# Loading a channel-mixing matrix as fp32 through SyncE in pieces of eight partitions, and rounding it on VectorE

## The chip, the core and the metric

The kernel runs on one core of one Trainium2 chip. The metric is the device time of one execution in microseconds (us). The kernel before takes 434.22 us, the median of three runs (433.93 to 435.81).

## What is computed

Two parts follow one another. The first is causal attention over 8 batches, 8 heads, 576 positions and 64 channels per head. Heads 0 to 3 see the last 32 positions, heads 4 to 7 every 32nd position. The second part takes the result as `x` (8 x 576 x 512), mixes its first 64 Fourier modes with one complex 512 x 512 matrix per mode, and then mixes channels with one real matrix, `w_ch`:

```python
X = np.fft.rfft(x, axis=1)                       # along the 576 positions
Yr = einsum('bmd,mde->bme', Xr, w_r) - einsum('bmd,mde->bme', Xi, w_i)
Yi = einsum('bmd,mde->bme', Xr, w_i) + einsum('bmd,mde->bme', Xi, w_r)
y = np.fft.irfft(Y, n=S, axis=1)                 # 64 modes, the others are zero
u = x + y
out = u + np.maximum(u @ w_ch, 0.0)
```

All inputs are fp32. `w_r` and `w_i` are 64 x 512 x 512 each, 64 MiB each. `w_ch` is 512 x 512, 1 MiB.

## The kernel before

The mode matrices are by far the largest input. They are fetched in halves of 256 input channels. One call fetches a half of two modes: two transfers issued by GpSimd, one for the real and one for the imaginary matrices, each of which reads 1 MiB of fp32 and writes 512 KiB of fp16 (the transfer rounds).

```python
GUEST = {1: "Y0", 2: "X0", 7: "YT"}   # pairs that live in the buffer of a later tile

def w_fetch(n=1):
    for _ in range(n):
        i = len(w_tiles)
        ...
        half, m = 1 - i // NM, i % NM
        if i // 2 in GUEST:
            wt = big.tile([128, 2, 4, DM], F16, tag=GUEST[i // 2], name="wt")
        else:
            wt = pw.tile([128, 2, 4, DM], F16, tag="w", name="wt")
        for ri, src in enumerate((moe_w_r, moe_w_i)):
            dst = wt[ds(64 * ri, 64)]
            ...                                   # one transfer for two modes
                nc.gpsimd.dma_start(dst, rows)
```

The buffer "YT" (8 KiB per partition) first holds weights of modes 14 and 15, and from the second half of the kernel on it holds sums of spectra. Between the two it is unused.

`w_ch` is fetched by one transfer of GpSimd, which also rounds to fp16:

```python
w_ch = big.tile([128, 4, DM], F16, name="w_ch")

def w_ch_fetch():
    nc.gpsimd.dma_start(w_ch, moe_w_ch.rearrange("(c p) e -> p c e", p=128))
    w_chs["n"] = w_ch
```

The inputs of attention come through GpSimd as well. The strided heads have 72 rows each time (4 heads x 18), which are loaded as 64 rows and 8 rows:

```python
def load_str(b, nb):
    for vi in (2, 0, 1):                          # v, q, k
        ...
        if nb == 2:
            nc.gpsimd.dma_start(two[0:64], src[0:64])
        else:
            nc.gpsimd.dma_start(ring[0:64, n, :], src[0:64, b % 2])
        if b % 2 == 0:
            nc.gpsimd.dma_start(two[64:72], src[64:72])   # 8 rows of two batches
```

The kernel has three stages. In the first, the strided heads are computed. In the second, the local heads of batch `b` are interleaved with the first halves of the modes, `NMODES[b]` of them per batch:

```python
NMODES = [11, 9, 8, 8, 7, 7, 7, 7]
for b in range(B):
    ...
    if b == 6:
        work.insert(0, w_ch_fetch)
    for mi in range(nm):
        ...                                       # some of the attention's work
        mode(0, sum(NMODES[:b]) + mi)             # 16 matmuls; every second fetches a pair
actx.close()
spectra_tile("YT")
```

In the third, the second halves of the modes run beside the channel mixing of `x`, and after the last mode the spectra are turned back and the outputs are written. `w_ch` is first read at the start of this third stage.

Of the kernel before, what the change touches and what calls it, by code (L numbers as in the profile page):

```python
# [10 lines left out]
FP = mybir.dt.float32  # L11
# [7 lines left out]
DM = 512  # L19
# [60 lines left out]
def kernel(  # L80
# [10 lines left out]
    nc = tc.nc  # L91
# [3 lines left out]
    big = ctx.enter_context(tc.tile_pool(name="big", bufs=1))  # L95
# [75 lines left out]
    w_chs = {}  # L171
    w_ch = big.tile([128, 4, DM], F16, name="w_ch")
# [27 lines left out]
            w_tiles.extend((wt[:, 0], wt[:, 1]))  # L200

    def w_ch_fetch():
        nc.gpsimd.dma_start(w_ch, moe_w_ch.rearrange("(c p) e -> p c e", p=128))
        w_chs["n"] = w_ch


# [26 lines left out]
    def load_loc(*bs):  # L233
        for b in bs:
            if b >= B:
                return
            for vi in (2, 0, 1):
                nc.gpsimd.dma_start(
                    loc_in(b, vi),
                    SRC[vi][b, 0:4].rearrange("h (cb i) d -> (h cb) (i d)", i=18),  # L240
                )
# [195 lines left out]
    def loc_scores(b, h, tail):  # L437
        par, hp = b % 2, h // 2
        scp = psum("sc")
        n, times = (256, 2) if tail else (160, 3)  # L440
        nc.tensor.matmul(  # L441
            scp[:, 0 : n * times].rearrange("p (h x) -> p h x", h=times),
            idn,
            mask_rows("cMl", n, times),
            start=True,
            stop=False,
        )
        todo = []
        if tail:
            for hh in range(2):  # L450
                todo.append((256 * hh, 576 * hh + 384, 160))
                todo.append((256 * hh + 192, 576 * hh + 512, 64))
        else:
            for t in range(3):
                todo.append((160 * t, 576 * (h % 2) + 128 * t, 160))
        for i, (col, s0, n) in enumerate(todo):
            nc.tensor.matmul(  # L457
                scp[:, ds(col, n)],
                kzs[par][:, hp, ds(s0, 128)],
                qTs[par][:, ds(s0, n)],  # L460
                start=False,
                stop=(i == len(todo) - 1),
            )
        PV = PL[:, 0:4096].rearrange("p (h x) -> p h x", h=4)
        if tail:
            dst = PV[:, ds(2 * hp, 2), 768:1024]
            src = scp.rearrange("p (h x) -> p h x", h=2)
        else:
            dst = PV[:, h, 0:768].rearrange("p (t x) -> p t x", t=3)[:, :, 0:160]
            src = scp[:, 0:480].rearrange("p (t x) -> p t x", t=3)  # L470
        nc.scalar.activation(out=dst, in_=src, func=ACTF.Exp, scale=SCALE)  # L471

    def loc_values(b, h):
        vg = v16[b % 2]
        av = psum("av")[:, 0:330].rearrange("p (t c) -> p t c", c=66)
        for t in range(5):
            off = 1024 * h + (256 * t if t < 4 else 960)
            nc.tensor.matmul(
                av[:, t, 0:65],
                PL[:, ds(off, 128)],  # L480
                vg[:, 2 * t + h % 2, v_cols(h // 2)],
                start=True,
                stop=(t == 0),
            )
            if t > 0:
                nc.tensor.matmul(  # L486
                    av[:, t, 0:65],
                    PL[:, ds(1024 * h + 256 * t - 128, 128)],
                    vg[:, 2 * (t - 1) + h % 2, v_cols(h // 2)],
                    start=False,  # L490
                    stop=True,
                )
        normalise(
            av[:, :, ds(1 - h // 2, 64)],
            av[:, :, 64 * (h // 2)],
            128,
            5,
            xb[b][:, 6:11, :].rearrange("p t (c h q) -> p t h c q", c=4, h=4)[:, :, h],
        )

    def dft(b, half):
        if half == 0 and b == 0:
            spectra_tile("X0")
        xp = psum("sc" if half else "y")
        tiles = (
            [(t, (JG[t % 3][1] - JG[t % 3][0]) * NCB) for t in range(6)]
            if half
            else [(t, SCS[t]) for t in range(5)]
        )
        F = cs["cFs"] if half else cs["cFl"]  # L510
        base = 0 if half else 6
        for cp in range(2):
            for i, (t, n) in enumerate(tiles):
                nc.tensor.matmul(  # L514
                    xp[:, ds(192 * cp, 192)].rearrange("p (f m) -> p f m", f=3),
                    xb[b][0:n, base + t, ds(128 * cp, 128)],
                    F[0:n, :, t, :],
                    start=(i == 0),
                    stop=(i == len(tiles) - 1),
                )  # L520
        xv = xp[:, 0:384].rearrange("p (c x) -> p c x", c=2)
        X = Xh[half]
        for src in range(2):
            for dst in range(2):
                args = dict(
                    out=X[ds(64 * dst, 64), ds(2 * src, 2), b].rearrange(
                        "p c g m -> p c (g m)"
                    ),
                    in_=xv[ds(64 * src, 64), :, ds(64 - 64 * dst, 128)],
                )  # L530
                act_copy(**args)
# [184 lines left out]
    def loc_front(b):  # L716
        if b >= B:
            return [lambda: None] * 8
        return [
            lambda: loc_turn(b, 0, 0), lambda: loc_turn(b, 0, 1),  # L720
            lambda: loc_turn(b, 1, 0), lambda: loc_turn(b, 1, 1),
            lambda: loc_turn(b, 2, 0), lambda: loc_turn(b, 2, 1),
            lambda: loc_back(b, 0), lambda: loc_back(b, 1),
        ]
# [3 lines left out]
    for i, w in enumerate(first):  # L728
# [10 lines left out]
        if i == 7:  # L739
            for n in ("cFs", "cFl"):  # L740
                nc.vector.tensor_scalar(
                    out=cs[n][:, 2], in0=cs[n][:, 0], scalar1=-1.0, scalar2=None,
# [32 lines left out]
    for b in range(B):  # L775
        load_loc(b + 6)
        front = loc_front(b + 1)
        scores = [lambda h=h: loc_scores(b, h, False) for h in range(4)]
        ends = [lambda h=h: loc_scores(b, h, True) for h in (0, 2)]
        values = [lambda h=h: loc_values(b, h) for h in range(4)]  # L780
        work = [
            scores[0], front[0], scores[1], ends[0], front[1], values[0], front[2],
            scores[2], front[3], values[1], scores[3], front[4], ends[1], front[5],
            values[2], front[6], values[3], front[7], lambda: dft(b, 0),
        ]
        if b == 6:
            work.insert(0, w_ch_fetch)
        n = 0
        nm = NMODES[b]
        for mi in range(nm):  # L790
            upto = -(-len(work) * (mi + 1) // nm)
            for w in work[n:upto]:
                w()
            n = upto
            mode(0, sum(NMODES[:b]) + mi)
# [12 lines left out]
    def w_turn(half, cp):  # L808
        wp = psum("sc")
        for c2 in range(2):  # L810
            for i in range(2):
                a = 64 * c2 + 32 * i
                nc.tensor.matmul(
                    wp[ds(a, 32), :],
                    idn.rearrange("p (x c) -> p c x", c=4)[:, 2 * cp + c2, :],
                    w_chs["n"][:, 2 * half + i, :],
                    start=True,
                    stop=True,
                    tile_position=(0, a),
                )  # L820
        act_copy(w_chs["cp"][:, 2 * half + cp, :], wp)

    work = [
        lambda half=half, cp=cp: w_turn(half, cp) for half in range(2) for cp in range(2)
    ]
# [149 lines left out]
    for i in range(len(units)):  # L975
        v_rows(i)
        b, t = units[i]
# [42 lines left out]
```

The softmax here doesn't subtract the row's maximum and nothing guards it: scores larger than these inputs give would overflow.

## Time and profile before

| | before |
|---|---|
| time, median of three | 434.22 us |
| PE / PEld busy | 78% / 56% of the span |
| DVE / ACT / POOL busy | 50% / 43% / 30% |
| DMA moved (as written) | 92.18 MB, mean 212 GB/s |
| HBM read / written | 163.22 MB / 9.44 MB |
| `w_ch` issued by GpSimd / landed after | 206.3 us / 20.1 us |
| `w_ch` first read by PE | 241.2 us |

PE is TensorE's matmuls, PEld its weight loads, DVE is VectorE, ACT ScalarE, POOL GpSimd and SP SyncE. The page counts DMA bytes as they are written, so a rounding transfer of 1 MiB of fp32 counts as 512 KiB. A queue's share in the page is the time of its packets as a share of 16 DMA engines over the span. A DMA reports its end once for each of the 16 engines; the trace keeps each of these completions and each packet with its time.

### The profile page before, as it was taken

How to read it: one execution, taken by the hardware profiler on the slowest of the kernel's cores; microseconds unless marked ns; L12 is line 12 of the kernel's file. 1: busy time of each engine (PE TensorE's matmuls, PEld its weight loads, DVE VectorE, ACT ScalarE, POOL GpSimd, SP SyncE). 2: the span in 40 equal slices, each digit the busy share in tenths (PEclk: the TensorE clock that was granted, in tenths of full speed). 3: DMA queues.
4: the chain of work that ended last, by engine and by line, in shares of the span. 5: the costliest groups of instructions: out<-in, count | busy, mean ns of one | idle time of the engine just before them, and what ended most of it. 6: DMA issues, size and time to landing. Idle time of an engine off the chain costs nothing.

```text
span 434.2 us, 12103 instructions
## 1 busy us (share of the span) xinstructions
PE 338.5 (78%) x5307; PEld 244.5 (56%) x5307; DVE 215.9 (50%) x468; ACT 187.5 (43%) x352; POOL 129.3 (30%) x208
## 2 busy tenths in 40 slices
PE   1986888779985787889885566587789798968993
PEld 1865776658864575667753344454456465643441
DVE  2888678744433243342511033355436366503894
ACT  1686678634643435444440401143215123602892
POOL 6433332322332222222222222222222221200992
PEclk9999899865985859875865569887958899988999
DMA  8999999999999999999999999999999999991787
GB/s 176 210 211 213 214 212 213 211 211 213 213 212 212 214 214 212 214 214 213 214 212 213 213 214 214 212 214 215 211 214 214 212 214 214 213 182 30 272 330 261
DMA packets 29140, 92.18 MB, mean 212 GB/s; under 512 B 4064, under 2 KB 5344, under 8 KB 29088
## 3 DMA queue, kind: packets, MB, share of 16 engines
q0 software_dynamic: 24704, 81.28, 94.4%
q1 hardware_dynamic: 3584, 9.59, 5.9%
q8 instruction: 42, 0.69, 0.6%
q10 hardware_dynamic: 800, 0.54, 0.5%
q14 instruction: 10, 0.08, 0.0%
HBM read 163.22 MB, written 9.44 MB: 398 GB/s over the span
## 4 chain that ended last, share of the span: by engine, by line
DMA 68%; PE 19%; DVE 6%; ACT 2%; issue 2%; POOL 1%; DVEq 0%; POOLq 0%
DMA wt<-in_moe_w_i_dram 51%; DMA wt<-in_moe_w_r_dram 11%; DMA ring<-in_q_dram 5%; PE y L547 2%; PE v L689 2%; DVE xb L250 2%; DVE kz L292 2%; PE u L689 2%; PE v L895 2%; PE sc L514 1%; ACT X L260 1%; PE tp L395 1%; DVE rec L249 1%; PE sc L441 1%; PE sc L353 1%
## 5 line engine op out<-in xcount | busy, mean ns | idle before, releaser
L547 PE MATMUL y<-X,wt 128*128 128x16 f16 (+1 forms) x2048 | 82.4, 192 | 61.0 <-DMA wt<-in_moe_w_i_dram 59.4
L547 PEld LDWEIGHTS <-wt 128*128 128x128 f16 (+1 forms) x2048 | 72.9, 103 | 76.5 <-issue 68.5
L196 POOL DMA_DIRECT2D wt<-in_moe_w_r_dram x62 | 36.5, 589 | 141.7 <-PE y L547 67.4
L196 POOL DMA_DIRECT2D wt<-in_moe_w_i_dram x60 | 35.4, 590 | 73.5 <-DMA wt<-in_moe_w_i_dram 61.2
L654 ACT ACTIVATE v<-sc 128x512 f16<-128x512 f32 x32 | 19.1, 597 | 69.7 <-PE sc L645 69.6
L645 PE MATMUL sc<-w_cp,xT 128*128 128x512 f16 (+1 forms) x160 | 48.2, 430 | 0.0
L471 ACT ACTIVATE PL<-sc 128x480 f16<-128x480 f32 (+1 forms) x48 | 27.3, 580 | 46.8 <-PE sc L457 46.5
L655 DVE COPY xo<-tp 128x512 f16<-128x512 f16 x32 | 22.1, 692 | 35.7 <-PE tp L653 35.6
L249 DVE RECIPROCAL rec<-av 90x4 f32<-90x4 f32 (+2 forms) x80 | 14.7, 184 | 46.2 <-PE av L486 34.8
L250 DVE TENSOR_TENSOR xb<-av,rec 90x256 f16<-90x256 f32 (+2 forms) x80 | 36.0, 450 | 2.7
L402 DVE COPY qT<-tp 128x576 f16<-128x576 f16 x16 | 12.0, 758 | 38.8 <-PE tp L395 35.9
L260 ACT ACTIVATE v<-tp 128x640 f16<-128x640 f16 (+1 forms) x24 | 19.4, 808 | 24.9 <-PE tp L429 22.1
L395 PE MATMUL tp<-cI_s,ring 64*64 64x64 f16 x864 | 26.7, 213 | 0.8 <-DVE qT L402 0.6
L360 ACT ACTIVATE PL<-sc 90x360 f16<-90x360 f32 (+1 forms) x48 | 22.7, 491 | 6.1 <-PE sc L353 5.3
L929 DVE TENSOR_TENSOR osb<-u,rl 128x512 f32<-128x512 f32 (+1 forms) x37 | 23.7, 674 | 1.8 <-PE u L689 1.1
L395 PEld LDWEIGHTS <-ring 64*64 64x64 f16 x864 | 21.1, 125 | 5.7 <-issue 2.6
L910 POOL TENSOR_TENSOR rl<-rl,xo 128x512 f32<-128x512 f32 x16 | 18.3, 1157 | 18.2 <-ACT rl L908 17.9
L441 PE MATMUL sc<-cMl_s,cI_s 128*128 128x480 f16 (+1 forms) x48 | 22.5, 468 | 1.6 <-ACT X L260 1.6
L457 PE MATMUL sc<-qT,kz 128*128 128x160 f16 (+1 forms) x160 | 22.4, 267 | 0.0
L908 ACT ACTIVATE rl<-v 128x512 f32<-128x512 f32 x36 | 20.4, 600 | 4.7 <-PE v L689 3.9
L285 PE MATMUL tp<-cI_s,ring 72*128 72x72 f16 x256 | 15.1, 206 | 9.4 <-DMA ring<-in_v_dram 7.9
L260 ACT ACTIVATE kz<-tp 64x360 f16<-64x360 f16 (+1 forms) x32 | 19.1, 595 | 7.7 <-PE tp L395 6.1
(103 smaller groups left out, 655.7 us busy)
## 6 DMA issues: line engine op xcount, KB each, us to landing
wt<-in_moe_w_r_dram POOLq DMA_DIRECT2D x62, 512.0 KB, 19.0
wt<-in_moe_w_i_dram POOLq DMA_DIRECT2D x60, 512.0 KB, 19.4
out_dram<-osb SPq DMA_DIRECT2D x14, 512.0 KB, 2.7
ring<-in_v_dram POOLq DMA_DIRECT2D x8, 288.0 KB, 13.3
ring<-in_q_dram POOLq DMA_DIRECT2D x8, 288.0 KB, 13.6
ring<-in_k_dram POOLq DMA_DIRECT2D x8, 288.0 KB, 13.5
ring<-in_v_dram POOLq DMA_DIRECT2D x3, 512.0 KB, 15.0
ring<-in_q_dram POOLq DMA_DIRECT2D x3, 512.0 KB, 14.8
```

Of the source, the lines that this page charges most:

```text
L196: nc.gpsimd.dma_start(dst, rows)
L250: nc.vector.tensor_tensor(out=dst, in0=val.rearrange("p h (q c) -> p h c q", c=4), in1=rec[0:n, 0:pieces] .to_broadcast((n, pieces, 64)) . ...
L260: nc.scalar.activation(out=out, in_=in_, func=ACTF.Copy)
L360: nc.scalar.activation(out=PS[0:n, ds(POFF[t], 4 * n)], in_=scp[0:n, 0 : 4 * n], func=ACTF.Exp, scale=SCALE,)
L395: nc.tensor.transpose(tp[ds(64 * hp, 64), ds(64 * i, 64)], qn[ds(64 * hp, 64), ds(64 * (9 * g + i), 64)], idn[ds(64 * hp, 64), ds(64 * hp, ...
L441: nc.tensor.matmul(scp[:, 0 : n * times].rearrange("p (h x) -> p h x", h=times), idn, mask_rows("cMl", n, times), start=True, stop=False,)
L457: nc.tensor.matmul(scp[:, ds(col, n)], kzs[par][:, hp, ds(s0, 128)], qTs[par][:, ds(s0, n)], start=False, stop=(i == len(todo) - 1),)
L471: nc.scalar.activation(out=dst, in_=src, func=ACTF.Exp, scale=SCALE)
L547: nc.tensor.matmul(yv[:, mi, e, :], wt[pr, XC[c], ds(128 * e, 128)], Xh[half][pr, c, :, :, m], start=(c == 0), stop=(c == 3),)
L645: nc.tensor.matmul(vp[pr, :], xT[:, ch, cols], w_chs["cp"][:, ch, :], start=(ch == 0), stop=(ch == 3),)
L655: nc.vector.tensor_copy(out=xo[pr].rearrange("p (h q c) -> p h q c", h=2, c=4), in_=tp[pr, 0:512].rearrange("p (h c q) -> p h q c", h=2, c=4),
L929: nc.vector.tensor_tensor(out=osb[:, t % 2, cols], in0=up[:, cols], in1=rls[b, t][:, t % 2, cols], op=AluOp.add,)
```

## The change

`w_ch` is no longer rounded on its way. SyncE loads it as fp32 in 16 transfers of eight partitions each, into the buffer "YT", which is unused at that time, at the start of batch 2 of the second stage instead of batch 6. VectorE rounds it into the fp16 tile at the start of batch 6. The transfer leaves the queue of GpSimd.

```diff
     def w_ch_fetch():
-        nc.gpsimd.dma_start(w_ch, moe_w_ch.rearrange("(c p) e -> p c e", p=128))
+        raw = big.tile([128, 4, DM], FP, tag="YT", name="w_raw")
+        rows = moe_w_ch.rearrange("(c p) e -> p c e", p=128)
+        for p in range(0, 128, 8):
+            nc.sync.dma_start(raw[ds(p, 8)], rows[ds(p, 8)])
+        w_chs["raw"] = raw
+
+    def w_ch_round():
+        nc.vector.tensor_copy(out=w_ch, in_=w_chs.pop("raw"))
         w_chs["n"] = w_ch
@@
+        if b == 2:
+            work.insert(0, w_ch_fetch)
         if b == 6:
-            work.insert(0, w_ch_fetch)
+            work.insert(0, w_ch_round)
```

## The prediction

> **What bounds the kernel now.** I read the page first, from its chain to its slices.
>
> ```profile
> DMA 68%; PE 19%; DVE 6%; ACT 2%; issue 2%; POOL 1%; DVEq 0%; POOLq 0%
> ...
> DMA  8999999999999999999999999999999999991787
> ...
> q0 software_dynamic: 24704, 81.28, 94.4%
> q1 hardware_dynamic: 3584, 9.59, 5.9%
> q8 instruction: 42, 0.69, 0.6%
> ```
>
> The first line is the chain that ended last, by engine: 68% is waiting for DMA, nearly all of it for mode matrices. The second is the DMA engines' busy share in 40 slices: full until slice 36 (about 390 us). The third to fifth are the queues. GpSimd's queue alone fills 94.4% of 16 engines' time; the fetching of instructions (q8) looks like nothing. So the kernel is one stream of weights of some 390 us and a tail of 40 us in which outputs are made. A saving counts only if it makes the stream end earlier.
>
> How does the stream end? The view of engines by stretches, asked in steps of 2 us. Its last two columns are the DMA share (16 engines are 1; overlapping packets bring it a little over) and GB/s:
>
> ```profile
> 384.00:386.00 2.00, 1.83 (x20) 1.02 (x21) 0.00 (x0) 0.00 (x0) 0.52 (x1) 0.60 1.05 209
> 386.00:388.00 2.00, 2.00 (x22) 0.98 (x21) 0.00 (x0) 0.00 (x0) 0.00 (x0) 0.54 0.95 191
> 388.00:390.00 2.00, 2.00 (x39) 1.41 (x38) 0.00 (x0) 0.00 (x0) 0.00 (x0) 1.00 0.54 107
> 390.00:392.00 2.00, 0.94 (x7) 0.20 (x3) 0.56 (x1) 0.00 (x0) 0.00 (x0) 1.00 0.55 109
> 392.00:394.00 2.00, 1.07 (x18) 0.61 (x18) 0.00 (x0) 0.00 (x0) 0.00 (x0) 1.00 0.17 33
> ```
>
> The share falls from 1.05 to 0.54, stays there for 4 us and then falls to nothing. **Half the engines are done some 5 us before the other half.** The completions of the very last weight transfer say the same, one per engine: eight at 387.5 to 389.2 us, eight at 392.8 to 393.9 us. TensorE waits for all sixteen, so the late eight set the end. In the third stage the gap of the two halves' means is 4.8 to 5.2 us from 360 us on.
>
> Why are eight late? Each of the 42 instruction packets (16 KiB) took 893 to 975 ns in most cases, and the durations repeat with a period of eight (893, 893, 948, 945, 935, 974, 974, 961 ns). I read this as a rotation over eight engines. By the page: 0.6% x 16 x 434 us is 42 us, and 42/8 is 5.2 us for each of eight engines and nothing for the rest. That is the gap. So the small q8 line is what the stream's end is made of.
>
> [...] GpSimd's 8-row loads agree: around each, eight engines show two data packets and eight none, and the halves alternate. [...]
>
> **The change part by part.**
>
> *Removed:* one transfer of GpSimd. 512 packets of 2 KiB read and 1 KiB written, 32 on each engine. In the completions, the step from one weight transfer to the next is 2.46 us, at `w_ch` 2.54 us. It lies on the stream, and all 16 engines get 2.54 us back. GpSimd's issue of 0.78 us was hidden: it runs some 19 us ahead of the landing (the issue list's medians are 19.0 and 19.4 us).
>
> *Added:* 16 transfers of 8 partitions, each 8 x 4 pieces of 2 KiB. [...] As fp32 I take 79 ns for a packet (2.54 us / 32, the same 2 KiB read) to 85 ns (the 2 KiB fp32 packets of the output's writes): 5.1 to 5.4 us on eight engines, 0 on the others. The net is +2.5 to +2.9 us on the eight that are chosen and -2.5 us on the others.
>
> *Moved:* the load goes from 206 us to about 116 us (mode 15, whose buffer it takes, runs at 115 to 117 us). The stream is full in both places (DMA share 1.07 at 105 to 125 us), so the place changes nothing in the sum. In between weights may land up to 5 us later than now on the loaded engines; GpSimd's lead of about eight transfers covers that, and it is made up before the end.
>
> *VectorE's rounding:* [...] 2.3 us at worst (the 128x512 fp32 sum takes 674 ns; four times its elements). At 195 to 205 us VectorE is busy for 3.39 of 10 us, and PE waits for weights there. Hidden. [...] SyncE has nothing else to do until the outputs.
>
> *Sum, if the chosen eight are the early ones:* early engines end at 389.2 + 2.7 = 391.9 us, late ones at 393.9 - 2.5 = 391.4 us. The stream ends 2.0 us earlier, perhaps 2.5 us if packets are cheap, and the tail of 40.3 us is unchanged: 434.2 - 2.3 = 431.9 us.
>
> **The rivals.**
>
> *A. The chosen eight include late engines.* Then the latest of them end at 393.9 + 2.7 = 396.6 us, and the time is 436.9 us. For it: by the packet records, engines that fetched instructions are found in both halves of the 8-row loads (the fetch at 46.7 us in one, those at 56.4 and 65.3 us in the other). [...] Against it: [...] the numbers fit too well: 1 MiB on half the engines is 5 us, which is the gap to be filled[...].
>
> *B. The pieces spread over all 16 engines* (by partition, say). Then each engine gets about what it lost, and the time stays at 434.2 us. [...]
>
> *C. VectorE's or GpSimd's new wait becomes the bound.* Then PE waits for attention's operands after 200 us. Idle time on VectorE and the queue's lead speak against it; it would make 1 us at most.
>
> *D. A second queue hides the load anyway* (gain of 2.5 us whatever the engines). Against it: a share of 1.06 leaves no room.
>
> **The range and the chances.** The main case I give 0.55, A 0.37, the others 0.08. The result has two likely places, about 431.9 and 436.9 us, each with a spread of half a microsecond. I put the number on the main case, and the range of 430.9 to 437.1 us has to hold both. Either is near 0.6% of the time, so within 2% is nearly certain: 0.96, with 0.02 on each side.
>
> **What the profile after would show.** Right: the fall from full to no DMA share at the end takes 2 us instead of 7, with no shelf at 0.54; the two groups of completions overlap; the last weight lands at 391 to 392 us; the HBM reads are unchanged, and q1 gains about 1 MB. A is right if the shelf is longer, with some engines ending at 396 us. B is right if the shelf is the same. The VectorE row for the rounding shows 1.2 or 2.3 us. It would be wrong altogether if the loads starve the attention stage, seen as a DMA share under 1 between 116 and 206 us, or if the tail changed.

## The result, and the profile after

The changed kernel takes 442.30 us, the median of five runs (440.87 to 442.62), where the kernel before takes 434.22 us. The ratio is 1.0156, with a 95% interval of 1.0132 to 1.0179; it is not the quotient of the two medians, which is 1.0186. It is slower by 7 to 8 us, two and a half to three times the 2.7 us that the worse rival had allowed, and outside the predicted range, though within the 2% that the prediction called nearly certain.

The page of the kernel after, its lines on the DMA engines' share in 40 slices, on the queues, and on the chain that ended last:

```profile
DMA  8999999999999999999999999999999999990786
...
q0 software_dynamic: 24176, 80.75, 93.1%
q1 hardware_dynamic: 4224, 10.64, 7.4%
q8 instruction: 42, 0.69, 0.6%
...
DMA 33%; PE 8%; issue 1%; DVE 0%; DVEq 0%; POOL 0%
```

Slice 37 now reads 0 where it read 1, but the slices are longer too and tell little. SyncE's queue (q1) has 640 packets more and its share is up by 1.5 points. That is 1.5% of 16 engines over 441 us, about 106 us, for data that was expected to cost 8 x 5.3 = 42 us. By the packet records, 84 us of it are the 512 data packets and 25 us the 128 packets of four bytes that report completions. This is the first sign of what went wrong. As predicted, the HBM reads are the same (163.22 MB) and q1 carries 1.05 MB more. The chain's 33% is not to be set against the 68% of before: the shares add up to 42%, so the chain was followed back over less than half the span.

The end of the stream, in the same view by stretches of 2 us (the last two columns are the DMA share and GB/s):

```profile
390.00:392.00 2.00, 0.00 (x0) 0.00 (x0) 0.00 (x0) 0.00 (x0) 0.44 (x1) 0.71 1.02 164
392.00:394.00 2.00, 1.76 (x20) 0.96 (x21) 0.00 (x0) 0.00 (x0) 0.51 (x1) 0.50 0.85 166
394.00:396.00 2.00, 2.00 (x21) 1.04 (x20) 0.00 (x0) 0.00 (x0) 0.00 (x0) 0.50 0.87 162
396.00:398.00 2.00, 2.00 (x22) 1.03 (x21) 0.00 (x0) 0.00 (x0) 0.00 (x0) 0.59 0.26 51
398.00:400.00 2.00, 1.71 (x22) 0.86 (x20) 0.56 (x1) 0.00 (x0) 0.00 (x0) 1.00 0.12 25
400.00:402.00 2.00, 1.07 (x18) 0.60 (x18) 0.00 (x0) 0.00 (x0) 0.00 (x0) 1.00 0.11 23
402.00:404.00 2.00, 1.85 (x22) 1.02 (x23) 0.29 (x1) 0.00 (x0) 0.00 (x0) 1.00 0.00 0
```

The shelf at 0.54 is gone, which the main case had as its sign, but not for its reason: the engines without extra work end late as well (see below). In its place is one at 0.12, and 2/16 is 0.125: **two engines work for 4 us alone.** The completions of the last weight transfer agree: fourteen between 396.0 and 397.6 us, two at 401.6 and 402.0 us. In the kernel before, the last was at 393.9 us. So the stream ends 8.1 us later, and the span, at 440.8 us, is 6.6 us longer than the 434.2 us of the profile before.

Where were the 8 us lost? The same view in steps of 10 us around the load:

```profile
125.00:135.00 10.00, 5.08 (x129) 3.98 (x126) 3.53 (x6) 3.14 (x7) 2.32 (x4) 0.82 1.17 188
135.00:145.00 10.00, 3.84 (x67) 2.83 (x67) 0.63 (x2) 2.27 (x4) 1.16 (x2) 0.50 1.15 199
...
155.00:165.00 10.00, 10.00 (x191) 7.45 (x191) 3.04 (x6) 4.53 (x9) 2.90 (x5) 0.64 1.06 213
```

In the first two of these stretches the kernel before shows:

```profile
125.00:135.00 10.00, 6.73 (x169) 5.37 (x167) 3.63 (x6) 3.72 (x8) 3.07 (x6) 0.84 1.07 214
135.00:145.00 10.00, 7.68 (x152) 6.22 (x153) 3.48 (x8) 4.26 (x7) 2.32 (x4) 0.65 1.07 214
```

Now the share is higher (1.17 against 1.07) while fewer bytes move (188 against 214 GB/s): SyncE's packets run beside GpSimd's, and by the packet records from 125 to 145 us GpSimd's packets of 4 KiB (as written) take 367 ns on average instead of 324 ns. TensorE pays for it between 120 and 160 us, in the view of waits for that stretch (total, times, longest, in us), first after and then before:

```profile
PE y L554 <- DMA wt<-in_moe_w_i_dram: 15.9, 3, 10.7
```

```profile
PE y L547 <- DMA wt<-in_moe_w_i_dram: 8.6, 5, 3.3
```

The other two parts of the change went as predicted. The view of the new tile (durations in ns, then the time of issue or start):

```profile
L206 SPq DMA_DIRECT2D w_raw<-in_moe_w_ch_dram x16: 272/280/387, 118.3 to 137.6; - x16
L210 DVE CAST w_ch<-w_raw x1: 1216/1216/1216, 209.3 to 209.3; 128x2048 f16<-128x2048 f32 x1
```

The rounding takes 1216 ns, and TensorE does not wait for it. GpSimd's issue at 209.65 us, begun during the rounding, took 0.99 us instead of 0.58 us and ended 0.1 us after the rounding. In five of the experiments an issue was held in the same way (1.27 to 1.57 us). GpSimd's lead of some 19 us (medians of 18.8 and 19.4 us from issue to landing) covers that. Each of the sixteen transfers shows eight completions as data lands, where a transfer of weights shows sixteen, and one other update at once. We read this as eight engines for each piece, and call the number of engines of a piece k: here k is 8.

### The profile page after: what moved, and what is told of

Its sections match the earlier page's. It is cut to its first block, busy times and chain, and to the rows that moved or that the text cites. A ratio compares the mean times of both kernels' runs of the same rounds, so it can differ in the third digit from the quotient of the medians.

```text
span 440.8 us, 12125 instructions
## 1 busy us (share of the span) xinstructions
PE 338.5 (77%) x5307; PEld 244.1 (55%) x5307; DVE 217.0 (49%) x469; ACT 187.7 (43%) x352; POOL 128.0 (29%) x207
## 3 DMA queue, kind: packets, MB, share of 16 engines
HBM read 163.22 MB, written 9.44 MB: 392 GB/s over the span
## 5 line engine op out<-in xcount | busy, mean ns | idle before, releaser
L409 DVE COPY qT<-tp 128x576 f16<-128x576 f16 x16 | 12.0, 758 | 42.2 <-PE tp L402 38.8
L267 ACT ACTIVATE v<-tp 128x640 f16<-128x640 f16 (+1 forms) x24 | 19.4, 808 | 22.0 <-PE tp L436 19.0
L402 PE MATMUL tp<-cI_s,ring 64*64 64x64 f16 x864 | 25.1, 205 | 1.6 <-issue 0.8
L464 PE MATMUL sc<-qT,kz 128*128 128x160 f16 (+1 forms) x160 | 23.4, 274 | 0.2 <-issue 0.2
L402 PEld LDWEIGHTS <-ring 64*64 64x64 f16 x864 | 19.5, 118 | 7.0 <-issue 4.5
L521 PEld LDWEIGHTS <-xb 108*128 108x128 f16 (+2 forms) x176 | 17.0, 115 | 10.9 <-DVE xb L257 5.7
L464 PEld LDWEIGHTS <-kz 128*128 128x128 f16 x160 | 16.6, 118 | 10.6 <-issue 8.0
## 6 DMA issues: line engine op xcount, KB each, us to landing
wt<-in_moe_w_r_dram POOLq DMA_DIRECT2D x62, 512.0 KB, 18.8
wt<-in_moe_w_i_dram POOLq DMA_DIRECT2D x60, 512.0 KB, 19.4
```

The costliest lines, as they stand in the source:

```text
L267: nc.scalar.activation(out=out, in_=in_, func=ACTF.Copy)
L402: nc.tensor.transpose(tp[ds(64 * hp, 64), ds(64 * i, 64)], qn[ds(64 * hp, 64), ds(64 * (9 * g + i), 64)], idn[ds(64 * hp, 64), ds(64 * hp, ...
L464: nc.tensor.matmul(scp[:, ds(col, n)], kzs[par][:, hp, ds(s0, 128)], qTs[par][:, ds(s0, n)], start=False, stop=(i == len(todo) - 1),)
```

## The experiments

Each kernel was timed beside the kernel before on the same chip, whose median was 435.08, 434.99 and 435.07 us for the three groups. Experiments 1, 7 and 8 are edits of the kernel before, the others of the changed kernel. The expectations of the first two groups name theories that fell. Their letters change in meaning: M is throughout some price of each packet beside the other queue's, P is a price of each piece or byte in experiment 4, and from experiment 9 on it says that the partitions that a piece writes set the price.

**1. What is the removed transfer worth?** `w_ch` is set to zero instead of being loaded; the channel mixing then adds nothing.

```diff
-        nc.gpsimd.dma_start(w_ch, moe_w_ch.rearrange("(c p) e -> p c e", p=128))
+        nc.vector.memset(w_ch, 0.0)
```

> Kernel before without the load of the channel weights (its tile is set to zero by VectorE, so the channel mixing is left out of the result). Says what the transfer is worth on the stream. If the stream sets the end on all engines: 2.5 us less than before, 431.7 us. If the transfer lies in a slack: as before, 434.2 us.

432.24 us, ratio 0.9933 (0.9908 to 0.9957). The last weights land at 391.4 us instead of 393.9. So the removal is worth the 2.5 us of the prediction, and a transfer on the stream costs its whole length.

**2. Sixteen partitions a piece instead of eight,** so that k is 16.

```diff
-        for p in range(0, 128, 8):
-            nc.sync.dma_start(raw[ds(p, 8)], rows[ds(p, 8)])
+        for p in range(0, 128, 16):
+            nc.sync.dma_start(raw[ds(p, 16)], rows[ds(p, 16)])
```

> The changed kernel with pieces of 16 partitions instead of 8, so that each piece lies on 16 engines. Theory M (a 2 KiB fp32 packet of SyncE costs some 150 ns among GpSimd's packets instead of 79): 32 packets per engine, 4.8 us, less the 2.5 us of the transfer that went: stream and time 2.3 us over before, 436.5 us, and the late engines' completions no more than 2.5 us later than before's. Theory C (only the concentration on eight engines is at fault, packets cost 79 ns): 434.2 us.

437.53 us, ratio 1.0046 (1.0028 to 1.0065). All sixteen engines lose about the same, 4.1 to 4.4 us, and the last weights land at 395.7 us. The packets of 2 KiB take 131 ns on average (165 ns in the changed kernel): dearer than the 79 to 85 ns of the prediction even without the choice of eight engines. Theory C falls.

**3. One transfer of fp32 by GpSimd,** at the same place.

```diff
-        for p in range(0, 128, 8):
-            nc.sync.dma_start(raw[ds(p, 8)], rows[ds(p, 8)])
+        nc.gpsimd.dma_start(raw, rows)
```

> The changed kernel with one fp32 transfer of 128 partitions by GpSimd in place of SyncE's sixteen, at the same place, rounded by VectorE too. Theory M (mixing two queues costs): no second queue, so as before, 434.2 us within 0.5. Theory F (writing fp32 instead of fp16 is what costs, whichever queue): 2 to 3 us over before.

436.53 us, ratio 1.0030 (1.0017 to 1.0044); the last weights land at 396.3 us. This is 1.3 us over before, between the two theories, and fits neither.

**4. Longer runs.** Each partition gets four adjacent rows, so it is filled by one packet of 8 KiB, not four of 2 KiB. The order of the input channels in the channel mixing differs from the reference's.

```diff
-        rows = moe_w_ch.rearrange("(c p) e -> p c e", p=128)
+        rows = moe_w_ch.rearrange("(p c) e -> p c e", p=128)
```

> The changed kernel, eight partitions at a time, but each partition gets four neighbouring rows, so that it reads one run of 8 KiB instead of four of 2 KiB (the order of the channels in the tile, and so the result, differs). Theory M (cost per packet in the mix): 16 packets of 8 KiB per engine at some 0.35 us, 5.5 us instead of 10: time some 4.5 us under the changed kernel, about 437 us. Theory P (cost per piece or per byte): no change, about 441 us.

445.37 us, ratio 1.0222 (1.0190 to 1.0254). The 8 KiB packets take 817 ns on average, 204 ns for 2 KiB. Neither theory had this. A fixed cost of each packet is ruled out as the main cost: with a quarter of the packets the load got dearer.

**5. One transfer of SyncE over all 128 partitions.**

```diff
-        for p in range(0, 128, 8):
-            nc.sync.dma_start(raw[ds(p, 8)], rows[ds(p, 8)])
+        nc.sync.dma_start(raw, rows)
```

> The changed kernel with one fp32 transfer of 128 partitions by SyncE instead of sixteen. Theory M (fp32 packets of a second queue cost 131 ns each among the weights' packets, however they are cut): as the eight pieces of 16, about 1.0046 of before, with every engine some 4 us later after it and 1.6 us later at the stream's end. Theory I (it is the number of pieces, each with its completion, that costs): as the one fp32 transfer by GpSimd, 1.003 or less.

435.14 us, ratio 0.9997 (0.9984 to 1.0010). Packets take 95 ns. A load through a second queue, as fp32, rounded by VectorE, thus costs what the old one did. Nothing in these three parts of the change is expensive; the cutting into pieces is. Why the same transfer costs a little more when GpSimd issues it (experiment 3) stays open.

**6. The pieces spread in time,** four at the start of each of the batches 2 to 5.

```diff
-        for p in range(0, 128, 8):
-            nc.sync.dma_start(raw[ds(p, 8)], rows[ds(p, 8)])
-        w_chs["raw"] = raw
+        w_chs["raw"], w_chs["rows"] = raw, rows
+
+    def w_ch_pieces(g):
+        nc.vector.memset(w_chs["raw"][ds(32 * g, 32), 0, 0:1], 0.0)
+        for i in range(4 * g, 4 * g + 4):
+            nc.sync.dma_start(w_chs["raw"][ds(8 * i, 8)], w_chs["rows"][ds(8 * i, 8)])
@@
+        if b in (2, 3, 4, 5):
+            work.insert(1 if b == 2 else 0, lambda g=b - 2: w_ch_pieces(g))
```

> The changed kernel with its sixteen pieces in four groups of four, one group each at the start of batches 2 to 5 of the second stage (a tiny VectorE memset of one column ahead of each group holds it back). Theory M (cost per packet, on eight engines of which two are late ones): the same, 1.0156 of before within 0.2%, and the loaded engines 10 us later in sum. Theory B (the burst is at fault: sixteen pieces in 35 us starve TensorE and GpSimd's queue): most of the 7 us is gone, under 1.008.

442.48 us, ratio 1.0159 (1.0133 to 1.0184), the same as with all pieces at once. So the burst is not the cause. (Of this kernel only the time is read.)

**7 and 8. Which engines are late?** The load stays GpSimd's own, rounding, in the old place, but cut into 76, 36 and 16 partitions. The author expected the 76 to load four engines, and the order of the first two pieces to change which four. No trace had shown this; the ends of the stream, below, agree with it for four engines and for three.

```diff
-        nc.gpsimd.dma_start(w_ch, moe_w_ch.rearrange("(c p) e -> p c e", p=128))
+        rows = moe_w_ch.rearrange("(c p) e -> p c e", p=128)
+        for p, n in [(0, 76), (76, 36), (112, 16)]:      # experiment 8: 36 rows first
+            nc.gpsimd.dma_start(w_ch[ds(p, n)], rows[ds(p, n)])
```

> Kernel before with its rounding load by GpSimd cut into 76, 36 and 16 partitions, in this order. [...] Theory E (engines that fetch instructions are late, the others early, and no second queue is needed to use that): if the four are early ones, they lose 6.1 - 2.5 = 3.6 us of their slack of 5 us, the twelve others gain 1.2 us, and the time is 1.2 us under before (0.997). If they are late ones, 3.6 us over before (1.008). If GpSimd spreads it over all 16 after all: as before.

> The same cuts in the order 36, 76, 16 partitions[...]. Theory E as before: 0.997 if these four are early engines, 1.008 if they are late ones; the completions of the last weights show which engines were loaded.

With the 76 first: 434.61 us, ratio 0.9994 (0.9980 to 1.0008). With them second: 440.19 us, ratio 1.0114 (1.0095 to 1.0134). The same bytes in the same pieces differ by 5.6 us by their order alone. The end of the stream with the 76 first:

```profile
386.00:388.00 2.00, 2.00 (x21) 0.99 (x20) 0.00 (x0) 0.00 (x0) 0.00 (x0) 0.62 0.86 172
388.00:390.00 2.00, 2.00 (x28) 1.10 (x24) 0.45 (x1) 0.00 (x0) 0.00 (x0) 1.00 0.81 160
390.00:392.00 2.00, 0.37 (x4) 0.06 (x3) 0.11 (x1) 0.00 (x0) 0.00 (x0) 1.00 0.72 143
392.00:394.00 2.00, 1.90 (x36) 1.12 (x36) 0.19 (x1) 0.00 (x0) 0.00 (x0) 1.00 0.14 27
```

The shelf is at 0.72 to 0.86 instead of 0.54: four early engines, now at 391.3 to 392.3 us, have come up beside the late eight (392.7 to 393.1 us), and only four are left idle (387.0 to 387.3 us). With the 76 second, three engines end at 399.3 to 399.4 us. So there are early and late engines; extra work on early ones cost nothing, and on late ones all of itself and more (the stream's end is 5.5 us later, where 3.6 us were expected), as the prediction had argued. But balance was worth little: the late eight ended 0.9 us earlier, and the time did not change measurably.

**9 to 12. Which side makes the packets slow?** What was left was that packets slow down as the partitions of a piece get fewer: 95 ns for 128, 131 for 16, 165 for 8. The few are also adjacent, so it may matter which partitions they are. To tell, the pieces were kept, with their number, size and k, and only their rows changed, to every fourth of 32: on both sides, on the side of the buffer alone, and on the side of HBM alone. In the last two, the order of the input channels differs from the reference's.

```diff
-        for p in range(0, 128, 8):
-            nc.sync.dma_start(raw[ds(p, 8)], rows[ds(p, 8)])
+        for p in range(16):
+            rws = slice(32 * (p // 4) + p % 4, 32 * (p // 4) + 32, 4)
+            nc.sync.dma_start(raw[rws], rows[rws])                  # both sides
+            # nc.sync.dma_start(raw[rws], rows[ds(8 * p, 8)])       # buffer alone
+            # nc.sync.dma_start(raw[ds(8 * p, 8)], rows[rws])       # HBM alone
```

> As the changed kernel, sixteen pieces of eight partitions by SyncE, but each piece takes every fourth partition of 32 (rows 0, 4, ... 28 and so on), both in memory and in the buffer; the rounding and the output stay the same. Theory P [...]: packets of 2 KiB fall from a mean of 165 ns to 95 to 105 ns, the loaded engines lose 6.1 to 6.7 us instead of 10.5, the last weights land at 397.3 to 398.3 us instead of 402.0, and the ratio to the kernel before is 1.007 to 1.010. Rival N (eight engines with two queues each is what costs, whatever the partitions): packets stay at 150 to 170 ns, ratio 1.014 to 1.017.

> Eight adjacent rows of the matrix are read by each piece, as in the changed kernel, but written to every fourth partition of the buffer (the order of the input channels of the channel mixing differs from the reference's by that). Theory P [...]: as with every fourth partition on both sides, packets of 95 to 105 ns, ratio 1.007 to 1.010. Rival H (where the rows lie in HBM is what costs): packets stay at 150 to 170 ns, ratio 1.014 to 1.017.

> The other half: each piece reads every fourth row of the matrix and writes it to eight adjacent partitions (the order of the input channels differs from the reference's by that). Theory P: packets stay at 150 to 170 ns, ratio 1.014 to 1.017. Rival H (place in HBM): packets of 95 to 105 ns, ratio 1.007 to 1.010.

| every fourth row | time | ratio (95%) | mean of a 2 KiB packet |
|---|---|---|---|
| on neither side (the change) | 442.30 us | 1.0156 (1.0132 to 1.0179) | 165 ns |
| on both sides | 438.20 us | 1.0088 (1.0056 to 1.0121) | 99 ns |
| in the buffer alone | 438.89 us | 1.0081 (1.0049 to 1.0114) | 103 ns |
| in HBM alone | 441.35 us | 1.0160 (1.0127 to 1.0193) | 162 ns |

The view of the DMA queues from 130 to 165 us shows it without any working on single packets (packets, MB, share of 16 engines). First the change, then every fourth row on both sides, then in the buffer alone, then in HBM alone:

```profile
q0 software_dynamic: 1787, 6.49, 97.6%
q1 hardware_dynamic: 428, 0.70, 13.5%
```

```profile
q0 software_dynamic: 1919, 6.99, 99.5%
q1 hardware_dynamic: 437, 0.71, 6.3%
```

```profile
q0 software_dynamic: 1908, 6.94, 99.2%
q1 hardware_dynamic: 428, 0.69, 7.2%
```

```profile
q0 software_dynamic: 1825, 6.65, 97.3%
q1 hardware_dynamic: 439, 0.72, 11.9%
```

The q1 lines carry nearly the same packets and megabytes, and their time falls by half when the buffer's partitions are spread, and by little when only the rows in HBM are. And q0, the weights, moves up to 0.5 MB more in the same 35 us. Which partitions are written decides (165 ns adjacent, 103 ns spread in the buffer alone). Why they do is shown by no trace.

One more thing differs: SyncE needs a median of 677 ns to issue a piece with spread partitions in the buffer (experiments 9 and 10), and 280 ns with adjacent ones (the change and experiment 11). The slower pace is not what shortens the packets. The whole load takes about as long either way (its packets start from 123.2 to 149.2 us in experiment 9, from 121.8 to 151.4 us in the change). And where at most three of its packets were under way at once, their means are 95 to 99 ns in experiment 9 and 140 to 160 ns in the change.

The end of the stream with every fourth row on both sides:

```profile
388.00:390.00 2.00, 2.00 (x22) 0.94 (x20) 0.00 (x0) 0.00 (x0) 0.03 (x1) 0.50 1.06 197
390.00:392.00 2.00, 2.00 (x22) 0.90 (x19) 0.00 (x0) 0.00 (x0) 0.00 (x0) 0.50 0.59 117
392.00:394.00 2.00, 2.00 (x32) 1.14 (x29) 0.00 (x0) 0.00 (x0) 0.00 (x0) 0.77 0.14 29
394.00:396.00 2.00, 0.85 (x4) 0.20 (x2) 0.56 (x1) 0.00 (x0) 0.00 (x0) 1.00 0.15 31
396.00:398.00 2.00, 1.79 (x36) 1.21 (x36) 0.04 (x1) 0.00 (x0) 0.00 (x0) 1.00 0.02 4
```

Fourteen engines are done by 393.0 us. The shelf of two engines (0.14, 0.15) is still there and ends at 397.2 us, 4.9 us earlier than in the change. This is the rest of the cost, and we put it down to the load lying on eight engines: with sixteen (experiment 12) it goes.

The last kernel does the same to pieces of sixteen: every fourth of 64 partitions.

```diff
-        for p in range(0, 128, 16):
-            nc.sync.dma_start(raw[ds(p, 16)], rows[ds(p, 16)])
+        for p in range(8):
+            rws = slice(64 * (p // 4) + p % 4, 64 * (p // 4) + 64, 4)
+            nc.sync.dma_start(raw[rws], rows[rws])
```

> Eight pieces of 16 partitions, all sixteen engines, each piece taking every fourth partition of 64 [...] instead of 16 adjacent ones [...], on both sides. Theory P: packets fall from a mean of 131 ns to 95 to 105 ns, all engines lose 3.1 to 3.5 us instead of 4.1 to 4.4 by the load, ratio 1.000 to 1.002 instead of 1.0046. Rival N (number of transfers under way): unchanged, 1.004 to 1.006.

435.41 us, ratio 1.0014 (0.9999 to 1.0028), with packets of 95 ns. The eight pieces now cost what the one transfer of experiment 5 does, to within the intervals.

**The sum with the measured packet.** The end of the last late engine is 393.9 us (before), less 2.5 us (removed), plus packets on one engine times their mean as the packet records have it (unrounded in the sum):

| kernel | packets x mean | worked out | last weights landed |
|---|---|---|---|
| the change | 64 x 165 ns | 401.9 us | 402.0 us |
| k = 8, every fourth row, both sides | 64 x 99 ns | 397.7 us | 397.2 us |
| the same, buffer alone | 64 x 103 ns | 398.0 us | 398.1 us |
| the same, HBM alone | 64 x 162 ns | 401.7 us | 400.5 us |
| k = 8, runs of 8 KiB | 16 x 817 ns | 404.5 us | 404.1 us |
| k = 16, adjacent | 32 x 131 ns | 395.6 us | 395.7 us |
| k = 16, every fourth row | 32 x 95 ns | 394.5 us | 394.9 us |
| one transfer | 32 x 95 ns | 394.5 us | 394.8 us |

One formula holds for eight kernels, to 1.2 us at worst and mostly to 0.5 us. It fits two others less well. If the 76 partitions of experiment 8 lie on four engines, that is 76 packets on each; at the mean of its own records, 118 ns, they alone give about 400.4 us, and 399.4 us was measured. Experiment 3 has 16 packets of 4 KiB at some 200 ns, which give 394.6 us, and 396.3 us was measured. The formula is a rule of thumb: packets overlap on an engine, so a packet's recorded time is not all taken from the others. The packets of the removed transfer have a mean of 98 ns in the records of before, while its landings come only 2.5 us, or 79 ns for each of 32, after those of the transfer ahead.

## Why the prediction was wrong

*The bound, and what a saving is worth: right.* One stream of weights and a tail; experiment 1 got back its 2.5 us.

*Late and early engines: right.* Experiments 7 and 8 show it. That instruction fetches make them late stays a reading of the numbers; no run took fetches away. In the profile before, the gap of the two halves' means grows steadily, from 0.2 us at the first transfer through 1.1 us at 74 us and 2.9 us at 200 us to 5.2 us. Eight engines that are a little slower throughout would look the same.

*Removed, eight engines, moved, rounded: right.* 2.5 us, k = 8 in the completions, 1216 ns hidden, and no effect of the place (experiment 6, and experiment 5 at the new place costs nothing). That all pieces lie on the same eight engines, 64 packets on each, was the author's assumption; no record names an engine. The sum above agrees with it: 401.9 us worked out, 402.0 us measured. One reading was off, without effect: at 195 to 205 us TensorE hardly waits for weights, as it is busy for 9.53 of 10 us there.

*Added, "As fp32 I take 79 ns for a packet": this step failed.* The figure came from transfers over all 128 partitions, and it was put on pieces of eight adjacent partitions. They measured 165 ns. So 64 packets cost 10.5 us instead of 5.1 to 5.4 us. This error is 5.2 us of the end of the stream, and experiments 9 to 12 show its cause: partitions on the buffer's side. Both figures were low even for spread partitions: 79 ns is a step between landings where the records of the same packets have 98 ns, and 85 ns is the median of the output's packets, whose mean is 109 ns. Spread, a packet of the load is 95 to 99 ns, so the term would be 6.1 to 6.3 us.

*Which eight: the main case failed here too, and rival A was right, with a twist.* We read the completions so that two of the eight that SyncE loads are late engines and six are early. The mark is the same in the five profiles with k = 8 that are read here: exactly two engines end last, 3 to 4 us after the next. At the prediction's own price of a packet this alone is the step from 431.9 to 436.9 us. Rival A's 436.9 us rested on packets of 79 to 85 ns; with 99 ns, experiment 9 gives 438.2 us. With 165 ns even eight early engines would have ended too late: 389.2 - 2.5 + 10.5 = 397.2 us, against the 393.9 us of before.

*The argument "the numbers fit too well" was misleading.* It took a purpose, read out of a coincidence of 5 us, for evidence on which engines are chosen. The trace spoke the other way: fetching engines were found in both halves.

*The lead of eight transfers does not cover the others.* The engines that carry nothing of `w_ch` should have ended at 386.7 us (early) and 391.4 us (late), 2.5 us sooner than before. They ended at 396.0 us and later. We take it that weights are asked for only as buffers come free, and that TensorE frees them at the pace of the slowest engine; no run tests this alone. From 135 to 160 us, right after the load, the first completion of a weight transfer came 2.3 to 2.5 us later than in the kernel before. As the prediction had a smaller imbalance in mind, it put this aside as made up before the end.

*DMA share under 1 as the sign of starvation: the wrong sign.* The share rose to 1.17 while the bytes fell (188 against 214 GB/s). Bytes, and TensorE's waits, show it.

*The tail was not a constant.* From the last weights to the end it is 40.2 us in the profile before, 38.8 us after, and 38.3 to 40.7 us in the profiles of the experiments. So the end of the stream gives the time only to about two microseconds; here that lessened the loss a little (6.6 us of span for 8.1 us of stream).

## What to carry to other kernels

When a load is cut into pieces, look at two things besides its bytes: on how many DMA engines a piece lands and which those are, and which partitions it writes. Adjacent partitions in small pieces made each packet 1.7 times as long here (165 against 99 ns), and every fourth partition, at the same number of pieces, gave that back. In this kernel, which is bound by a stream over all engines, one transfer over all partitions was as good as the best cut (ratios 0.9997 and 0.9994). Take the duration of a packet from a transfer of the same shape, and in one measure (a step between landings, or recorded durations), or treat it as unknown.

## What was not expected of the hardware

- Beside the full stream of weights, the recorded time of a 2 KiB packet depends on the partitions that its transfer writes: 95 ns over 128 partitions, 131 ns over 16 adjacent, 165 ns over 8 adjacent, 95 to 103 ns over every fourth.
- Longer runs did not help: 817 ns for 8 KiB, 204 ns for each 2 KiB, on eight adjacent partitions.
- The engines are not equally late (the last weights before: eight at 387.5 to 389.2 us, eight at 392.8 to 393.9 us), and SyncE's eight seem to be of both kinds: by the completions, two late engines are among them, and the order of two pieces of GpSimd's load was worth 5.6 us (434.61 against 440.19 us).
- One engine's delay seems to spread to all through TensorE's wait: all engines, those without an extra packet too, ended at 396.0 us or later, 5 to 9 us after the 391.4 and 386.7 us that their own work asked for.
